# Retention, PReLU layer and mixture of experts on one core: the head's state update moved to TensorE and ScalarE, float32 products regrouped, the update cut to its diagonal blocks, and the first slot's weights given a later due time

## The chip, the core and the metric

The kernel runs on one core of a Trainium2 chip. The metric is the device time of one execution in microseconds (us); of the kernel before there are three timed runs, with a median of 981.19 us (980.25 to 981.85). One further execution was taken with the hardware profiler. TensorE is called PE here, VectorE DVE, ScalarE ACT, GpSimd POOL and SyncE SP; SP issues nearly all DMAs.

## What is computed

Three stages follow each other over 3072 tokens (4 batches of 768) with 512 features.

```
state = gamma_h * state + outer(k_t, v_t)            # per batch and head: 4 x 8 states of 64 x 64, float32
y_t   = scale * q_t @ state                          # decaying linear attention, 768 steps
h     = x @ w_in ; g = max(h,0) + alpha*min(h,0)     # 512 -> 2048
x2    = g @ w_out                                    # 2048 -> 512
e     = argmax(cosine(x2, expert_emb)/tau)           # 8 experts, top 1
out   = gate * (max(x2 @ w1[e], 0) @ w2[e])          # 512 -> 1024 -> 512, only the chosen expert
```

## The kernel before, in words

**Tiles.** The tokens are cut into 24 tiles of 128, numbered i = 4c + b: chunk c (0 to 5) of batch b (0 to 3). The recurrence is done by chunks. For each tile `att_load` fetches q, k, token-major k and v, and with each new chunk the decay factors `cqk_sb`; `att_hat` multiplies the decays in; `att_a` makes the masked scores (eight float32 products, one for each head, over 64 rows); `att_b` makes the output `y` = scores x v plus q x state (the second part only from chunk 1 on), and the update `u` = k^T v, which DVE adds to the state `st_bd`. The state lies as four 128 x 128 blocks for each batch, one for each pair of heads, of which only the two 64 x 64 blocks on the diagonal are used. `u` is computed for a pair of heads at once, four float32 products of 128 x 128, so half of each (the two blocks of one head's k with the other's v) is not read. `y` and `u` take turns in two PSUM banks (`m_ring`).

**Two kinds of tile.** Tiles 0 to 11 (`i < HALVED`) make scores x v in float32. Tiles 12 to 23 split scores and v into two float16 halves (`att_s`, three products in place of one); q x state stays float32, with the scaled state `st_y`. In `y` of these tiles the order by pair of heads is: six float16 products, one float32 product, and the next pair.

**Stages.** Called the head here: tiles 0 to 11, the conversion of the two PReLU matrices (they come in as 64-bit numbers, `convert`, `quarter`, `scale_out`, `split_out`) and the first block of h = x w_in (`mm1(0, m)`). Then the middle: blocks of 512 tokens through `mm1` and `mm2`, with tiles 12 to 23 and the splitting of the expert weights into float16 halves (written to `wsplit` in HBM) in between. In the last block the 128-token groups end one after the other; each is squared, halved (`Route.halve`), transposed by a DMA into `x2T_buf` (`Route.logits`) and multiplied with the expert embedding `emb16` on PE. After that come the expert slots: four fixed ones (t = -4 to -1, of the two most frequent experts) and then t = 0, 1, ... The weights of the slots lie in three buffers: t = -4, -3 in `stage16`, t = -2, -1 in `win16`, t = 0 in `wout16`, t = 1 in `stage16`, and so on. `load_w(t)` fetches them in four pieces of 1 MB.

**Order.** No order is written by hand. Every call is recorded (`Plan.add`; all instructions of the program are therefore issued from one line, L147) with an estimated duration (`cost`) and its dependencies. `Plan.issue` gives every node a due time `need`, counted back from the place of the PE work that depends on it, and then fills the engines' in-order queues greedily: of what can start first, the one due first. A DMA is held back until its `need` is within `AHEAD` = 60 us of the PE work just placed. `plan.bias` is added to the `need` of what is recorded under it. The added lines of the change stand in `cost`, `att_load`, `att_b`, the setup and the calls of `load_w`.

Of the kernel before, what the change touches and what calls it, by code (L numbers as in the profile page):

```python
# [14 lines left out]
AF = mybir.ActivationFunctionType  # L15
ALU = mybir.AluOpType
AX = mybir.AxisListType

B, H, S, D = 4, 8, 768, 64
NT, DM, DFF = B * S, H * D, 2048  # L20
E, F = 8, 1024
P = 128
# [5 lines left out]
KD = DM // P  # L28
# [68 lines left out]
class Plan:  # L97
# [37 lines left out]
    class Engine:  # L135
# [26 lines left out]
        def cost(self, method, kw):  # L162

            n = 1
            for d in kw["out"].shape[1:]:
                n *= d
            if "dma" in method:
                side = kw["in_"] if "indirect" not in method or kw["in_offset"] is None else kw["out"]
                n = 1
                for d in side.shape:  # L170
                    n *= d
                nb = n * mybir.dt.size(side.dtype)
                if "indirect" in method:
                    return 1040.0, 650.0, nb
                return 60.0, (1150.0 if "transpose" in method else 1000.0), nb * (1.23 if "transpose" in method else 1)
            if self.name == "PE":
                if kw["lhsT"].dtype == F32:
                    return max(214.0, 1.67 * n), 0.0, 0
                return max(27.0, 0.416 * n + 2.5), 0.0, 0
            if self.name == "ACT":  # L180
                extra = sum(93.0 for k in ("accum_out", "scale", "bias") if isinstance(kw.get(k), bass.AP))
                return (95.0 if kw["in_"].space != bass.MemoryType.PSUM else 50.0) + 0.833 * n + extra, 0.0, 0
            if self.name == "DVE":
                fast = method in ("tensor_scalar", "tensor_copy") and n > 64 and kw.get("op0") not in self.BITS
                two = method in ("scalar_tensor_tensor", "tensor_tensor") and n > 256
                return 65.0 + n * (0.52 if fast else 1.05) * (1.15 if two else 1.0), 0.0, 0
            return 140.0 + (2.13 if method == "tensor_tensor" else 1.3) * n, 0.0, 0
# [139 lines left out]
def retention_prelu_moe_kernel(ctx: ExitStack, tc, qkv, w_in, w_out, alpha, emb, tau, w1, w2,  # L327
                               c32, cqk, causal, c16, out):
    nc = tc.nc
    plan = Plan(nc)  # L330
    V, A, G, T, SP = plan.vector, plan.scalar, plan.gpsimd, plan.tensor, plan.sync
# [10 lines left out]
    def buf(name, shape, dt=F32):  # L342
        return sbuf.tile([P, *shape], dt, name=name, tag=name)
# [18 lines left out]
    cst = buf("cst", [NCOL])  # L362
    cst16 = buf("cst16", [2 * P + E], F16)
    cau = buf("cau", [P])
    alpha_sb = buf("alpha_sb", [KF])
    tau_sb = buf("tau_sb", [1])
    cqk_sb = buf("cqk_sb", [2, KD, P])

    def col(name):
        return cst[:, _COLS[name][0]:_COLS[name][1]]  # L370

    tri, ones16, base16 = cst16[:, 0:P], cst16[:, P:2 * P], cst16[:, 2 * P:]
# [14 lines left out]
    v_ring = Ring([vp_buf[:, k] for k in range(2)])  # L387
# [4 lines left out]
    first = {"qk": [room[:, 1536 * k:1536 * k + 1536].rearrange("p (a x) -> p a x", a=3) for k in range(3)] + [qk_buf, hat_buf, stage[:, 12:15]],  # L392
             "v": [room[:, 4608 + 512 * k:5120 + 512 * k] for k in range(2)] + v_ring.bufs,
             "pm": [room[:, 5632 + 512 * k:6144 + 512 * k].rearrange("p (k t) -> p k t", k=KD) for k in range(4)] + pm_ring.bufs,
             "xh": [room[:, 7680 + 512 * k:8192 + 512 * k].bitcast(F16).rearrange("p (a x) -> p a x", a=2) for k in range(3)] + xh_ring.bufs,
             }
    first = {k: Ring(v) for k, v in first.items()}
# [76 lines left out]
    qk_t, v_t, att = {}, {}, {}  # L474

    def att_load(i):
        if i % B == 0:
            SP.dma_start(out=cqk_sb, in_=cqk[i // B])
        qk_t[i] = (first["qk"] if i < B * N_ROOM else qk_ring).next() if i < HALVED else qk_buf
        SP.dma_start(out=qk_t[i], in_=qkv[i, :, 0:3])  # L480
        v_t[i] = (first["v"] if i < B * N_ROOM else v_ring).next()
        SP.dma_start(out=v_t[i], in_=qkv[i, :, 3])

    def att_hat(i):
# [77 lines left out]
    def att_b(i, early=False):  # L562

        c, b = divmod(i, B)
        j, o = divmod(i, BT)
        v = v_t.pop(i)
        hat, pr = att.pop(i)
        st = st_bd[:, b]
        y = m_ring.next()
        with plan.unit("PE"):  # L570
            for p in range(KD):
                for r in range(2):
                    h = 2 * p + r
                    if i >= HALVED:
                        for n, (a, o_) in enumerate(((0, 0), (0, 1), (1, 0))):
                            T.matmul(out=y[:, D * h:D * h + D], lhsT=p16[r][:, a, P * p:P * p + P],
                                     rhs=v16[:, o_, D * h:D * h + D], start=(r == n == 0), stop=False, skip_group_check=True)
                        continue
                    T.matmul(out=y[:, D * h:D * h + D], lhsT=pr[r][:, p, :], rhs=v[:, D * h:D * h + D],
                             start=(r == 0), stop=(r == 1 and not c), skip_group_check=True)  # L580
                if c:
                    T.matmul(out=y[:, P * p:P * p + P], lhsT=hat[:, 0, P * p:P * p + P], rhs=(st_y if i >= HALVED else st)[:, p, :],
                             start=False, stop=True, skip_group_check=True)
        if c < NCH - 1:
            u = m_ring.next().rearrange("p (k t) -> p k t", k=KD)
            with plan.unit("PE"):
                for p in range(KD):
                    T.matmul(out=u[:, p, :], lhsT=hat[:, 2, P * p:P * p + P], rhs=v[:, P * p:P * p + P],
                             start=True, stop=True)
        xh = (first["xh"] if i < B * N_ROOM else xh_ring).next()  # L590
        ss = tmp("ssx", [1])
        square_sum(y, ss, xh[:, 0, :])
        if c < NCH - 1:
            for r in (0, D):
                V.tensor_tensor(out=st[r:r + D, :, r:r + D], in0=u[r:r + D, :, r:r + D],
                                in1=st[r:r + D, :, r:r + D], op=ALU.add)
        s = tmp("sx", [1])
        pow2(ss, s, C_WIDE, hbx[:, i:i + 1])
        if o == BT - 1:
            pow2_inverse(hbx[:, i + 1 - BT:i + 1], invx[:, i + 1 - BT:i + 1], C_WIDE)  # L600
            for k in range(i + 1 - BT, i + 1):
                if k in y_inv:
                    for q in range(2):
                        V.tensor_tensor(out=invx[:, k:k + 1], in0=invx[:, k:k + 1], in1=y_inv[k][:, q:q + 1], op=ALU.mult)
        A.activation(out=xh[:, 0, :], in_=y, func=AF.Copy, scale=s)
        V.scalar_tensor_tensor(out=xh[:, 1, :], in0=y, scalar=s, in1=xh[:, 0, :], op0=ALU.mult, op1=ALU.subtract)
        if early:
            SP.dma_start(out=x_dram[i], in_=xh.rearrange("p a x -> p (a x)"))
        else:
            att_x(i, xh.rearrange("p a x -> p (a x)"))  # L610
# [376 lines left out]
    SP.dma_start(out=tau_sb, in_=tau.partition_broadcast(P))  # L987
    SP.dma_start(out=emb_sb, in_=emb)
    V.memset(st_bd, 0.0)
    V.memset(csum, 0.0)  # L990
    V.memset(ss_b, 0.0)
    V.memset(ones_b, 1.0)
# [207 lines left out]
    def load_w(t):  # L1200

        for piece in range(4):
            which, o = divmod(piece, 2)
            dst = wbuf(t)[:, 4 * piece:4 * piece + 4].rearrange("p c a x -> p (c a x)")
            cols = slice(4096 * o, 4096 * o + 4096)
            if t in (0, 1):

                SP.dma_start(out=dst, in_=wsplit[(E - 1) * t, which][:, cols])
                continue
            which_e = pre_e[t >= -NPAIR][0:1, 0:1] if t < 0 else ctl[0:1, 0, t:t + 1]  # L1210

            def load(which=which, dst=dst, which_e=which_e, cols=cols):
                ev = nc.sync.value_load(which_e, min_val=0, max_val=E - 1)
                kw = {}
                if t > 1:
                    kw = dict(cond=nc.sync.value_load(ctl[0:1, 1, t:t + 1], min_val=0, max_val=1), cond_hint=False)
                src = wsplit[bass.ds(ev, 1), which].rearrange("a p x -> p (a x)")
                nc.sync.dma_start(out=dst, in_=src[:, cols], **kw)

            plan.add("SP", load, [which_e, ctl[0:1, 1, t:t + 1], wsplit] if t > 1 else [which_e, wsplit], [dst], 250.0, 1000.0,  # L1220
                     P * 4096 * (1 if t > 1 else 2))
# [42 lines left out]
                             in_=y, in_offset=None, bounds_check=NT - 1, oob_is_err=False)  # L1264

    for t in (-NPRE, -NPAIR, 0):
        load_w(t)
    for first_t in (-NPRE, -NPAIR):
        for t in range(first_t, first_t + NPAIR):
            mm1e(t)  # L1270
        for t in range(first_t, first_t + NPAIR):
            mm2e(t)
# [84 lines left out]
```

## Time and profile before

| | before |
|---|---|
| median of the timed runs | 981.19 us (980.25 to 981.85) |
| the profiled execution | 988.65 us, span 986.9 us |
| mean granted clock of PE | 0.966 |
| busy share of the span: PE, DVE, ACT, POOL | 94 %, 58 %, 47 %, 9 % |
| HBM read, written | 200.40 MB, 51.14 MB |

The span runs from the first to the last instruction. A busy time of an engine is the time in which it carried out instructions; the PE's float32 products appear as two matmul records each, each with a load of weights of its own (PEld). A granted clock of 1.00 is 2.4 GHz and 0.50 is 1.2 GHz. "idle before ... <- X" is how long the engine stood still before an instruction and what released it.

### The profile page before, as it was taken

How to read it: one execution, taken by the hardware profiler on the slowest of the kernel's cores; microseconds unless marked ns; L12 is line 12 of the kernel's file. 1: busy time of each engine (PE TensorE's matmuls, PEld its weight loads, DVE VectorE, ACT ScalarE, POOL GpSimd, SP SyncE). 2: the span in 40 equal slices, each digit the busy share in tenths (PEclk: the TensorE clock that was granted, in tenths of full speed). 3: DMA queues.
4: the chain of work that ended last, by engine and by line, in shares of the span. 5: the costliest groups of instructions: out<-in, count | busy, mean ns of one | idle time of the engine just before them, and what ended most of it. 6: DMA issues, size and time to landing. Idle time of an engine off the chain costs nothing. (4 is left out here: it accounts for less than half of the span.)

```text
span 986.9 us, 18868 instructions
## 1 busy us (share of the span) xinstructions
PE 926.3 (94%) x7100; PEld 558.7 (57%) x7100; DVE 571.3 (58%) x1490; ACT 464.6 (47%) x825; POOL 91.4 (9%) x110
## 2 busy tenths in 40 slices
PE   6797789999999999999998999997999999989995
PEld 6775455555555555554444444446677677666663
DVE  5988989578787877796466557446422222121231
ACT  1568866577687778887576664222001101100100
POOL 0000000000200010001000100110232112132010
PEclk9797979999999999999999999998999999989998
DMA  9998723564899888888686543797687279945450
GB/s 306 305 266 254 239 102 89 161 159 119 261 277 233 221 269 269 235 229 291 197 236 229 192 156 100 298 261 153 219 195 188 72 222 341 311 114 111 63 196 25
DMA packets 129823, 201.44 MB, mean 204 GB/s; under 512 B 89726, under 2 KB 90110, under 8 KB 124608
## 3 DMA queue, kind: packets, MB, share of 16 engines
q1 hardware_dynamic: 123168, 179.42, 62.1%
q0 software_dynamic: 6560, 20.77, 6.5%
q8 instruction: 57, 0.93, 0.4%
q14 instruction: 38, 0.31, 0.1%
HBM read 200.40 MB, written 51.14 MB: 255 GB/s over the span
## 5 line engine op out<-in xcount | busy, mean ns | idle before, releaser
L147 PE MATMUL bank<-xT,win 128*128 128x512 f16 x1152 | 270.7, 386 | 7.0 <-DVE g L147 7.0
L147 PE MATMUL bank<-wout,f_buf 128*128 128x512 f16 x960 | 223.4, 381 | 0.8 <-DVE pay_buf L147 0.8
L147 PEld LDWEIGHTS <-win 128*128 128x128 f16 x1344 | 123.3, 100 | 136.9 <-issue 15.7
L147 PEld LDWEIGHTS <-f_buf 128*128 128x128 f16 x960 | 93.1, 98 | 110.9 <-issue 4.0
L147 PEld LDWEIGHTS <-stage 128*128 128x128 f16 x1440 | 89.3, 98 | 26.8 <-issue 4.2
L147 DVE SCALAR_TENSOR_TENSOR g<-g,oma,bank 128x512 f32<-128x512 f32 x96 | 71.4, 745 | 55.3 <-ACT g L147 54.6
L147 ACT ACTIVATE wout<-stage 128x1024 f16<-128x1024 f32 x64 | 67.3, 1052 | 39.2 <-DMA stage<-in_w 38.6
L147 ACT ACTIVATE st_bd<-bank 128x512 f16<-128x512 f32 x30 | 17.9, 597 | 140.5 <-PE bank L147 126.8
L147 ACT ACTIVATE g<-bank 128x512 f32<-128x512 f32 x96 | 56.4, 588 | 57.0 <-PE bank L147 56.7
L147 DVE SCALAR_TENSOR_TENSOR f_buf<-g,f_buf 128x512 f16<-128x512 f32 x80 | 55.1, 689 | 32.9 <-ACT f_buf L147 32.4
L147 POOL DMA_INDIRECT table<-pay_buf,rposi x24 | 25.6, 1066 | 473.3 <-DVE v L147 112.7
L147 PEld LDWEIGHTS <-wout 128*128 128x128 f16 x1152 | 65.9, 98 | 5.2 <-issue 2.2
L147 PEld LDWEIGHTS <-st_bd 128*128 128x128 f16 x408 | 39.8, 99 | 47.6 <-issue 2.5
L147 ACT ACTIVATE f_buf<-g 128x512 f16<-128x512 f32 x80 | 49.8, 623 | 29.0 <-DVE g L147 28.9
L147 DVE SCALAR_TENSOR_TENSOR stage<-stage,se 128x1024 f16<-128x1024 f32 x43 | 55.0, 1280 | 8.4 <-ACT stage L147 8.4
L147 PE MATMUL bank<-xT,stage 128*128 128x128 f16 x960 | 56.8, 220 | 3.2 <-issue 3.2
L147 PE MATMUL bank<-xT,wout 128*128 128x128 f16 x960 | 56.5, 220 | 1.8 <-issue 1.8
L147 DVE SCALAR_TENSOR_TENSOR st_bd<-bank,st_bd 128x512 f16<-128x512 f32 x34 | 23.3, 689 | 55.0 <-ACT st_bd L147 50.3
L147 ACT ACTIVATE stage<-stage,se 128x1024 f16<-128x1024 f32 x43 | 48.8, 1139 | 9.6 <-DMA wsplit<-stage 5.7
L147 DVE TENSOR_SCALAR xT<-bank,f_buf,cqk_sb 128x512 f32<-128x512 f32 x20 | 16.2, 810 | 62.4 <-PE bank L147 62.4
L147 PEld LDWEIGHTS <-x2T_buf 128*128 128x128 f16 x384 | 26.9, 99 | 34.1 <-DMA x2T_buf<-pay_buf 8.0
L147 PE MATMUL bank<-wout,stage 128*128 128x512 f16 (+1 forms) x200 | 44.6, 375 | 0.0
(263 smaller groups left out, 1257.8 us busy)
## 6 DMA issues: line engine op xcount, KB each, us to landing
stage<-wsplit SPq DMA_DIRECT2D x52, 1024.0 KB
wout<-wsplit SPq DMA_DIRECT2D x52, 1024.0 KB
stage<-in_w SPq DMA_DIRECT2D x64, 512.0 KB
wsplit<-stage SPq DMA_DIRECT2D x43, 512.0 KB
qk_buf<-in_qkv SPq DMA_DIRECT2D x15, 768.0 KB
wsplit<-win SPq DMA_DIRECT2D x21, 512.0 KB
f_buf<-in_w_in SPq DMA_DIRECT2D x12, 512.0 KB
vp_buf<-in_qkv SPq DMA_DIRECT2D x20, 256.0 KB
```

Of the source, the lines that this page charges most:

```text
L147: call = lambda: fn(**kw)
```

## The change

Five edits, in the order of the diff.

- The planner's estimates for float32 products on PE are set anew; they decide about order alone.
- A tile `ident` (128 x 128 identity) is made from the two triangles `cau` and `tri`, both loaded anyway.
- `att_load`: up to tile 11 only the half of the decay factors that is used there is fetched (256 KB in place of 512 KB, for chunks 0, 1 and 2); for tile 0, q and k come first, then the factors, v, and last the token-major k.
- `att_b`: for tiles 12 to 23 the four float32 products with the state stand together behind all float16 products. The update is made as eight products of 64 x 64, each head's own block. For tiles 4 to 11, a product of `ident` with the old state (128 x 512, float32) opens the update's bank, so that the sum forms in PSUM, and ACT copies the blocks to `st_bd`; for tiles 0 to 3 (state zero) ACT copies `u` alone. Tiles 12 to 19 keep DVE's addition; tiles 20 to 23 have no update.
- `load_w(0)` is recorded with a bias of 15 us.

```diff
-                    return max(214.0, 1.67 * n), 0.0, 0
+                    rows, cols = kw["lhsT"].shape[0], kw["lhsT"].shape[1]
+                    return (145.0 if rows < P else 100.0 if cols < P else 120.0 + 1.17 * n), 0.0, 0
...
     def att_load(i):
-        if i % B == 0:
-            SP.dma_start(out=cqk_sb, in_=cqk[i // B])
+        if i % B == 0 and i:
+            n = 1 if i < HALVED else 2
+            SP.dma_start(out=cqk_sb[:, 0:n], in_=cqk[i // B][:, 0:n])
...
+        if i == 0:
+            SP.dma_start(out=qk_t[i][:, 0:2], in_=qkv[i, :, 0:2])
+            SP.dma_start(out=cqk_sb[:, 0:1], in_=cqk[0][:, 0:1])
+            SP.dma_start(out=v_t[i], in_=qkv[i, :, 3])
+            SP.dma_start(out=qk_t[i][:, 2], in_=qkv[i, :, 2])
+            return
...
-                if c:
-                    T.matmul(out=y[:, P * p:P * p + P], lhsT=hat[:, 0, P * p:P * p + P], rhs=(st_y if i >= HALVED else st)[:, p, :],
+                if 0 < c and i < HALVED:
+                    T.matmul(out=y[:, P * p:P * p + P], lhsT=hat[:, 0, P * p:P * p + P], rhs=st[:, p, :],
+                             start=False, stop=True, skip_group_check=True)
+            if i >= HALVED:
+                for p in range(KD):
+                    T.matmul(out=y[:, P * p:P * p + P], lhsT=hat[:, 0, P * p:P * p + P], rhs=st_y[:, p, :],
                              start=False, stop=True, skip_group_check=True)
...
-                for p in range(KD):
-                    T.matmul(out=u[:, p, :], lhsT=hat[:, 2, P * p:P * p + P], rhs=v[:, P * p:P * p + P],
-                             start=True, stop=True)
+                add = 0 < c and i < HALVED
+                if add:
+                    T.matmul(out=u.rearrange("p k t -> p (k t)"), lhsT=ident, rhs=st.rearrange("p k t -> p (k t)"),
+                             start=True, stop=False, skip_group_check=True)
+                for h in range(H):
+                    p, r = divmod(h, 2)
+                    T.matmul(out=u[D * r:D * r + D, p, D * r:D * r + D], lhsT=hat[:, 2, D * h:D * h + D],
+                             rhs=v[:, D * h:D * h + D], start=not add, stop=True, skip_group_check=True)
...
-                V.tensor_tensor(out=st[r:r + D, :, r:r + D], in0=u[r:r + D, :, r:r + D],
-                                in1=st[r:r + D, :, r:r + D], op=ALU.add)
+                if i < HALVED:
+                    A.activation(out=st[r:r + D, :, r:r + D], in_=u[r:r + D, :, r:r + D], func=AF.Copy)
+                else:
+                    V.tensor_tensor(out=st[r:r + D, :, r:r + D], in0=u[r:r + D, :, r:r + D],
+                                    in1=st[r:r + D, :, r:r + D], op=ALU.add)
...
+    V.tensor_tensor(out=ident, in0=cau, in1=tri, op=ALU.subtract)
...
     for t in (-NPRE, -NPAIR, 0):
+        plan.bias = 15000.0 if t == 0 else 0.0
         load_w(t)
+    plan.bias = 0.0
```

## Rows read from the trace of the kernel before

**Rows 1.** Stages by windows: stretch, length, busy time of each engine (instructions), clock, DMA share, GB/s

```profile
0.00:40.00 40.00, 27.59 (x180) 25.80 (x182) 25.58 (x53) 13.11 (x21) 0.39 (x5) 0.87 0.93 299
40.00:68.00 28.00, 25.77 (x214) 20.81 (x211) 26.08 (x48) 15.43 (x24) 0.00 (x0) 1.00 1.09 332
68.00:148.00 80.00, 62.78 (x347) 39.96 (x347) 70.41 (x115) 64.13 (x94) 0.42 (x3) 0.83 0.58 189
160.00:640.00 480.00, 476.17 (x2884) 241.65 (x2883) 339.32 (x906) 324.87 (x603) 27.64 (x39) 1.00 0.71 214
```

**Rows 2.** Timeline of PE, 205 to 230 us: start, busy us, operation, count

```profile
208.03 0.34 PE L147 MATMUL bank<-v,p 128*128 128x64 f16 x6
...
208.20 0.47 PE L147 MATMUL bank<-st_y,hat_buf 128*128 128x128 f32 x2
...
209.94 1.46 PE L147 MATMUL bank<-wout,stage 128*128 128x512 f16 x6
...
214.57 1.16 PE L147 MATMUL bank<-hat_buf 64*128 64x128 f32 x16
...
215.66 1.47 PE L147 MATMUL bank<-wout,stage 128*128 128x512 f16 x6
...
220.90 1.05 PE L147 MATMUL bank<-vp_buf,hat_buf 128*128 128x128 f32 x8
...
221.79 0.81 PE L147 MATMUL bank<-wout,stage 128*128 128x512 f16 x3
```

**Rows 3.** Groups of PE by form, 160 to 640 us: busy us, mean ns, idle before

```profile
L147 PE MATMUL bank<-st_y,hat_buf 128*128 128x128 f32 x96 | 22.4, 316 | 0.0
```

**Rows 4.** The tile st_bd: its DVE additions, duration ns min/median/max, first and last

```profile
L147 DVE TENSOR_TENSOR st_bd<-bank,st_bd x40: 404/427/456, 18.8 to 335.2; 64x256 f32<-64x256 f32 x40
```

**Rows 5.** Stages by windows, instructions of the tile st_bd alone

```profile
40.00:68.00 28.00, 7.04 (x32) 4.86 (x32) 2.50 (x6) 0.00 (x0) 1.00 1.09 332
68.00:148.00 80.00, 8.85 (x32) 6.31 (x32) 4.25 (x10) 0.00 (x0) 0.83 0.58 189
```

**Rows 6.** Groups of ACT by form, 0 to 160 us

```profile
L147 ACT ACTIVATE g<-bank 128x512 f32<-128x512 f32 x17 | 10.0, 589 | 6.5 <-PE bank L147 6.4
```

**Rows 7.** DMA issues by line: form, count, KB each

```profile
cqk_sb<-in_cqk SPq DMA_DIRECT2D x6, 512.0 KB
```

**Rows 8.** Timeline of PE, 133 to 168 us: the first product with wout

```profile
154.40 2.75 PE L147 MATMUL bank<-wout,stage 128*128 128x512 f16 x12
```

**Rows 9.** Timeline of PE, 655 to 723 us

```profile
654.78 9.23 PE L147 MATMUL bank<-wout,f_buf 128*128 128x512 f16 x42
...
669.96 0.38 PE L147 MATMUL bank<-emb,x2T_buf 128*128 128x16 f16 x8 [5.95 <-DMA x2T_buf<-pay_buf]
...
670.20 5.44 PE L147 MATMUL bank<-wout,f_buf 128*128 128x512 f16 x15
...
686.05 0.35 PE L147 MATMUL bank<-emb,x2T_buf 128*128 128x16 f16 x8 [1.38 <-DMA x2T_buf<-pay_buf]
...
722.34 5.58 PE L147 MATMUL bank<-xT,wout 128*128 128x128 f16 x96
```

**Rows 10.** Timeline of SP's queue, 651 to 668 us: issue, time to issue

```profile
652.63 0.53 SPq L147 DMA_DIRECT2D wout<-wsplit  x1
...
655.93 0.39 SPq L147 DMA_DIRECT2D wout<-wsplit  x1
...
658.93 3.65 SPq L147 DMA_TRANSPOSE x2T_buf<-pay_buf  x1
...
662.68 5.15 SPq L147 DMA_TRANSPOSE x2T_buf<-pay_buf  x1
```

**Rows 11.** Stages by windows, one microsecond each

```profile
664.00:665.00 1.00, 0.01 (x1) 0.00 (x0) 0.30 (x2) 0.00 (x0) 0.00 (x0) 1.00 1.02 434
```

**Rows 12.** Timeline, 597 to 606 us: an earlier pair of transposes and its first user

```profile
599.48 5.32 SPq L147 DMA_TRANSPOSE x2T_buf<-pay_buf  x2
...
603.19 0.34 PE L147 MATMUL bank<-emb,x2T_buf 128*128 128x16 f16 x8
```

More of the change, by code (lines that the diff above doesn't have):

```diff
@@ L364, in retention_prelu_moe_kernel @@
     cau = buf("cau", [P])
+    ident = buf("ident", [P])
     alpha_sb = buf("alpha_sb", [KF])
@@ L476, in att_load @@
     def att_load(i):
-        if i % B == 0:
-            SP.dma_start(out=cqk_sb, in_=cqk[i // B])
+        if i % B == 0 and i:
+            n = 1 if i < HALVED else 2
+            SP.dma_start(out=cqk_sb[:, 0:n], in_=cqk[i // B][:, 0:n])
         qk_t[i] = (first["qk"] if i < B * N_ROOM else qk_ring).next() if i < HALVED else qk_buf
+        v_t[i] = (first["v"] if i < B * N_ROOM else v_ring).next()
+        if i == 0:
[4 more added lines that the diff above has]
+            return
         SP.dma_start(out=qk_t[i], in_=qkv[i, :, 0:3])
-        v_t[i] = (first["v"] if i < B * N_ROOM else v_ring).next()
         SP.dma_start(out=v_t[i], in_=qkv[i, :, 3])
@@ L576, in att_b @@
                             T.matmul(out=y[:, D * h:D * h + D], lhsT=p16[r][:, a, P * p:P * p + P],
-                                     rhs=v16[:, o_, D * h:D * h + D], start=(r == n == 0), stop=False, skip_group_check=True)
+                                     rhs=v16[:, o_, D * h:D * h + D], start=(h == n == 0), stop=False, skip_group_check=True)
                         continue
```

## The prediction, made before the changed kernel was built or run

> **What bounds the kernel now.** I read the stages first [rows 1]: one line for each stretch, with the busy time of every engine. From 160 to 640 us PE is busy for 476.17 of 480 us at full clock, so there any time taken off PE's instructions comes off the end. From 68 to 148 us no engine is full: DVE has 70.41 of 80 us, ACT 64.13, PE 62.78 at a mean clock of 0.83. DVE is the fullest, so its work counts first there. From 40 to 68 us DVE (26.08 of 28 us) and the DMA share (1.09) are both at their end; before 40 us it is the DMAs (0.93), with DVE at 25.58 of 40 us. The head ends where the first product with wout starts, at 154.40 us [rows 8]. The last place is the passage to the expert slots. In PE's timeline [rows 9] the reader is to see that PE runs out of work at about 664 us, stands for 5.95 us until a transposed x2T_buf arrives, and then takes 5.44 us for 15 matmuls of a form of which 42 took 9.23 us just before.
>
> **The change, part by part.**
>
> *Float32 state products side by side (tiles 12 to 23).* Today one unit of y, with four times six float16 and one float32 product, runs from 208.03 to 209.94 us: 1.91 us [rows 2]. Its first six float16 products take 208.20 - 208.03 = 0.17 us, so 0.68 us for all 24, and the four float32 ones with their changes of type have 1.23 us. The update, four float32 products of the same size side by side, takes 221.79 - 220.90 = 0.89 us [rows 2]. So each change of type costs (1.23 - 0.89)/4 = 0.085 us; of four, three go: 0.25 us for a tile. The 96 records of st_y are twelve tiles of eight [rows 3], all inside the full stretch: 12 x 0.25 = **3.0 us**. It is 0 if the extra time belongs to the operands and not to the change, and 12 x 0.34 = 4.1 us if the last change is hidden too.
>
> *Only the own blocks of the update.* No row has a product of 64 columns of weights with 64 columns moving. If the eight run one after the other, each at half of a 0.2225 us product (0.89/4), they take 0.89 us, as now; if the two halves of the array work side by side, 0.45 us. The scores use half arrays in the other direction: eight products with 128 columns moving take 215.66 - 214.57 = 1.09 us [rows 2], 1.22 times the 0.89 us of perfect pairs. So 0.45 x 1.22 = 0.55, and I add 0.2 us for going into and out of the halved array, about twice one change of type: 0.75 us, nearest to the scores' row. Gain 0.14 us for a tile, counted for the eight tiles 12 to 19 in the full stretch: **1.1 us**; bounds 8 x (0.89 - 1.09) = -1.6 and 8 x 0.44 = +3.5 us. The Trainium skill, page "TensorEngine Tiling (Array Packing)", section "Key Properties", speaks against it: a change of tiling mode, not of tile, drains TensorE. No row here shows a drain by itself; if drains ate the gain, the sum below would be 1.1 us smaller.
>
> *The state's addition moved (tiles 0 to 11).* DVE loses 24 of its 40 additions of 427 ns [rows 4]: 10.2 us in all, of which 2.50 lie in 40 to 68 us and 4.25 in 68 to 148 us [rows 5]. ACT gains 24 copies of 64 x 256 from PSUM. A copy of 512 elements takes 589 ns [rows 6]; half of it (0.29) and all of it bound the new one, I take 0.38, since part of each instruction does not depend on its length. PE gains eight products with ident, each 512 float32 columns: 4 x 0.2225 = 0.89 us at full clock, 1.78 at half; at least the 0.22 us of one float16 pass over 512 columns (9.23/42) [rows 9]. The wait that it adds, for the state as ACT left it four tiles before, q x state of the same tile has already; what is new stands behind ACT's queue and not DVE's (a rival below). For 68 to 148 us, with five tiles: DVE 70.41 - 4.25 = 66.2, ACT 64.13 + 10 x 0.38 = 67.9, PE 62.78 + 5 x (0.89 - 0.14) = 66.5 us. The fullest engine falls from 70.4 to 67.9 us, by 2.5 us; but three engines are then about equal and each waits for the others, so I take 1.5 us.
>
> *The DMAs of the first 68 us.* Three loads of decay factors shrink by half of 512 KB [rows 7]: 0.79 MB less, at 332 GB/s [rows 1] 2.4 us of the queues' time. With the 2.50 us that DVE loses in 40 to 68 us it is one gain, not two, since both are full there; I take 2.0 us. Tile 0 starts earlier, as 0.52 MB (half the factors and the token-major k) no longer stand before its first product: 1.7 us at the 299 GB/s of 0 to 40 us. SP issues one DMA more for it, 0.39 to 0.53 us of its queue by the plain loads of [rows 10]. The stream behind it is bound by bytes, so 0.5 us is left. The making of ident is one more DVE instruction, smaller than an addition of the state, in a stretch where DVE has 14 us idle.
>
> The head together: 1.5 + 2.0 + 0.5 = **4.0 us**. Bounds: 8 x 0.75 = 6.0 us of loss, if PE's added work all stands in the way and nothing else helps, and 10.2 us of gain, if all that DVE loses counts. The new estimates reorder the head's queues; I have no row for that, and leave it inside these bounds.
>
> *The first slot's weights later.* SP issues two of the four pieces, 1 MB each, at 652.63 and 655.93 us; two transposes follow at 658.93 and 662.68 and take 3.65 and 5.15 us to issue [rows 10]. The DMAs still move 434 GB/s from 664 to 665 us [rows 11], loads and not transposes. The earlier pair, with no loads ahead, had its first user 603.19 - 599.48 = 3.7 us after the first issue [rows 12]; the later one 669.96 - 658.93 = 11.0 us. Due 15 us later, the two pieces come behind this pair: 2.1 MB at 434 GB/s are 4.9 us less. A stall of about 1 us is left, between none (658.93 + 3.7 lies before 664) and 2.1 us (if the second transpose, whose data are ready 3.5 us after the first's, counts). With so short a stall the clock stays up: 5.44 - 15 x 0.22 = 2.1 us come back. **7.0 us**. The four are plain DMAs with nothing else on SP. They are needed from 722.34 us on [rows 9]; 15 us later than 655.93 leaves 50 us, so that end is covered. What they can hit is the next pair of transposes, where PE waits 1.38 us today [rows 9]: if all four pieces now stood ahead of it, 4.9 us would be lost again. Bounds 2.1 and 5.95 + 2.1 = 8.1 us. The Trainium skill, page "DMA: Bandwidth & Descriptors", section "Where 436 GB/s comes from", puts loads from HBM at about 358 GB/s for a core. The trace differs with its 434 GB/s, and the measurement decides; by the page's figure the pieces would be worth 5.9 us and the sum would be 1 us larger.
>
> **Sum.** 3.0 + 1.1 + 4.0 + 7.0 = 15.1 us. The profiled execution took 988.65 us and would take 973.5; it is 7.5 us above the median of 981.19 us, and I take the same gain off that: **966 us**.
>
> **Rivals.**
> - *The loads hit the transposes all the same* (that edit doesn't do what it says). For it: the planner fills SP's queue whenever a load may go, and the second pair of transposes follows closely. Against: 15 us is longer than the 11.0 us from the first issue to its user. The gain of 7.0 us goes: 973 us.
> - *The head gives nothing.* ACT and PE get what DVE loses, and three engines at 66 to 68 of 80 us wait for one another. 970 us. Both together: 977 us.
> - *The head gives all of DVE's time*, 10.2 us in place of 4.0: 960 us. Against it stands the DMA share of 1.09 in 40 to 68 us.
> - *Slower.* The update's bank is one of two that all tiles share, and it now comes free when ACT has copied it. PE's queue is in order, so a product for that bank holds everything behind it. Price for each of the tiles 4 to 11: 0.89 for ident, 0.76 for two copies, 0.59 for one ACT instruction ahead of them, 2.24 us, 17.9 us in all, against 11.1 us from the other parts: 988 us. It decides from (11.1 + 2)/8 = 1.6 us a tile. Against it: PE has 17 us idle in 68 to 148 us, and DVE, which frees the bank today, is the fuller engine.
>
> **How the numbers follow.** Forecast 0.48, loads hit the transposes 0.15, head gives nothing 0.17, both 0.05, head gives all 0.07, slower 0.08. The range 957 to 977 us takes in every case but the slower one and the outer halves of its neighbours. 0.2 % is 2 us, about what a measurement of this kernel can tell from no change: faster 0.88, same 0.04 (the upper part of "both"), slower 0.08.
>
> **What would show it.** In y of tiles 12 to 23: 24 float16 products and then eight float32 records, 1.65 us in place of 1.91. An update of about 0.75 us, and in tiles 4 to 11 before it a 128 x 512 float32 product of 0.9 us. The first product with wout near 150 us. Loads of wout from wsplit behind the first two transposes of x2T_buf, a stall below 2 us there, and no stretch at half clock after it. I am wrong if the first product with wout is not earlier, or if the stall only moves to the second pair.

## The result, and the profile after

The changed kernel takes **972.93 us** (median of four runs, 970.79 to 975.04); the kernel before, run beside it, 981.52 us (980.25 to 985.52). The ratio is **0.9888** with a 95 % interval of [0.9855, 0.9922]: faster by 1.1 %, inside the forecast's range, but by 8.6 us where 15.1 were forecast. Two more groups of runs on other chips gave 0.9863 [0.9834, 0.9892] and 0.9889 [0.9854, 0.9924], which is 13.2 and 11.8 us. Executions more than 1.5 % above the fastest of their kernel are left out of medians and ratios.

The profiled execution took 975.04 us, its span is 973.3 us. First its stages, in the columns and stretches of [rows 1] (length, busy time of PE, PEld, DVE, ACT, POOL with their counts, clock, DMA share, GB/s):

```profile
40.00:68.00 28.00, 25.62 (x206) 18.03 (x205) 20.99 (x38) 18.10 (x30) 0.00 (x0) 0.94 0.97 292
68.00:148.00 80.00, 67.95 (x438) 40.77 (x437) 70.81 (x119) 68.67 (x109) 2.71 (x3) 0.91 0.59 198
160.00:640.00 480.00, 475.79 (x2972) 237.50 (x2971) 337.45 (x901) 323.85 (x602) 35.79 (x44) 1.00 0.71 217
```

From 160 to 640 us PE is as full as before: what it saves there shows as later work coming earlier, not as idle time. From 40 to 68 us DVE fell from 26.08 to 20.99 us and the DMA share from 1.09 to 0.97. From 68 to 148 us DVE did not fall: though ten additions of the state are gone from it [rows 5], it has 119 instructions in place of 115, so work that used to come later has moved up, and PE rose from 62.78 to 67.95 us.

PE's timeline of the same kernel (start, busy us, operation, count), in order the product with ident, the first product with wout, an update, and a unit of y; they answer to [rows 2, 8]:

```profile
122.85 1.02 PE L147 MATMUL bank<-st_bd,ident 128*128 128x512 f32 x2
123.81 0.69 PE L147 MATMUL bank<-vp_buf,qk_buf 128*64 128x64 f32 x16
...
147.37 5.34 PE L147 MATMUL bank<-wout,stage 128*128 128x512 f16 x24
...
198.73 0.69 PE L147 MATMUL bank<-vp_buf,hat_buf 128*64 128x64 f32 x16
199.35 2.76 PE L147 MATMUL bank<-xT,win 128*128 128x512 f16 x12
201.95 0.86 PE L147 MATMUL bank<-v,p 128*128 128x64 f16 x24
202.65 1.14 PE L147 MATMUL bank<-st_y,hat_buf 128*128 128x128 f32 x8
203.62 2.10 PE L147 MATMUL bank<-wout,stage 128*128 128x512 f16 x9
```

A unit of y now takes 203.62 - 201.95 = 1.67 us, the update 199.35 - 198.73 = 0.62, the ident product 123.81 - 122.85 = 0.96. ScalarE's copies of the state, as a group (busy us, mean ns, idle before):

```profile
L147 ACT ACTIVATE st_bd<-bank 64x256 f32<-64x256 f32 x24 | 9.0, 376 | 2.6 <-PE bank L147 2.4
```

Now the passage to the expert slots. PE's timeline after, to be held against [rows 9] (in brackets the idle time before, and what ended it):

```profile
658.66 0.37 PE L147 MATMUL bank<-emb,x2T_buf 128*128 128x16 f16 x8 [4.45 <-DMA x2T_buf<-pay_buf]
658.89 5.75 PE L147 MATMUL bank<-wout,f_buf 128*128 128x512 f16 x15
...
675.38 0.35 PE L147 MATMUL bank<-emb,x2T_buf 128*128 128x16 f16 x8 [1.70 <-DMA x2T_buf<-pay_buf]
...
710.09 2.12 PE L147 MATMUL bank<-xT,wout 128*128 128x128 f16 x35
```

and SP's queue after, against [rows 10] (issue, time to issue):

```profile
644.46 0.36 SPq L1245 DMA_DIRECT2D win<-wsplit  x1
644.86 0.43 SPq L147 DMA_DIRECT2D wout<-wsplit  x1
646.13 0.34 SPq L1245 DMA_DIRECT2D win<-wsplit  x1
646.57 0.45 SPq L147 DMA_DIRECT2D wout<-wsplit  x1
649.14 8.40 SPq L147 DMA_TRANSPOSE x2T_buf<-pay_buf  x2
```

The stall is still there, and so are the 15 slow matmuls: 5.75 us, with a granted clock of 0.57 over them, mostly the lower of the two levels. By windows (columns as in the stages above):

```profile
658.90:664.50 5.60, 5.60 (x22) 2.07 (x19) 3.82 (x29) 1.77 (x5) 0.00 (x0) 0.57 0.54 187
```

The reason stands in SP's queue: two pieces of the first slot's weights (the rows named wout; those named win are weights of the slots before) still go out ahead of the transposes, at 644.86 and 646.57.

To see where the time went I cut each trace at three marks: the first product with wout, the moment at which PE runs out of work before the first emb product (its start less its idle time), and the first product of slot 0 (bank<-xT,wout). I use two profiled executions of the kernel before (span 986.9 us, and a second one, 980.3) and three of the changed one (973.3, 968.4, 973.1), since single executions differ by some microseconds:

| stretch, us | before | mean | after | mean | gain | forecast |
|---|---|---|---|---|---|---|
| head, to the first wout product | 154.4, 152.9 | 153.7 | 147.4, 145.9, 146.9 | 146.7 | 7.0 | 4.0 |
| middle, to PE out of work | 509.6, 509.4 | 509.5 | 506.8, 504.0, 504.6 | 505.2 | 4.3 | 4.1 |
| passage, to slot 0 | 58.3, 55.5 | 56.9 | 55.9, 54.8, 58.5 | 56.4 | 0.5 | 7.0 |
| slots, to the end of the span | 264.6, 262.5 | 263.5 | 263.2, 263.7, 263.1 | 263.4 | 0.1 | 0 |

The middle is as forecast, the head gave more, the passage next to nothing. The gains add up to 11.9 us and not to 8.6, because these are five single executions; the three groups of timed runs gave 8.6, 13.2 and 11.8 us.

### The profile page after: what moved, and what is told of

It is laid out like the page before. It is cut to its first block, busy times and chain, and to the rows that moved or that the text cites. A ratio compares the mean times of both kernels' runs of the same rounds, so it can differ in the third digit from the quotient of the medians.

```text
span 973.3 us, 19219 instructions
## 1 busy us (share of the span) xinstructions
PE 922.6 (95%) x7276; PEld 548.5 (56%) x7276; DVE 561.1 (58%) x1467; ACT 471.9 (48%) x849; POOL 97.6 (10%) x110
## 5 line engine op out<-in xcount | busy, mean ns | idle before, releaser
L147 PE MATMUL bank<-xT,win 128*128 128x512 f16 x1152 | 266.9, 382 | 6.9 <-DVE g L147 6.9
L147 ACT ACTIVATE st_bd<-bank 128x512 f16<-128x512 f32 (+1 forms) x54 | 26.9, 499 | 141.6 <-PE bank L147 127.1
L147 POOL DMA_INDIRECT table<-pay_buf,rposi x24 | 28.6, 1194 | 443.3 <-DVE f_buf L147 122.8
L147 PE MATMUL bank<-xT,stage 128*128 128x128 f16 x960 | 56.4, 219 | 2.2 <-issue 2.2
L147 PE MATMUL bank<-wout,st_bd 128*128 128x512 f16 x192 | 45.8, 397 | 0.8 <-issue 0.8
L147 ACT ACTIVATE x2T_buf<-bank 128x512 f16<-128x512 f32 x14 | 8.4, 597 | 75.2 <-PE bank L147 52.7
```

Source lines behind the costliest of these rows:

```text
L147: call = lambda: fn(**kw)
```

## The experiments

They ran in three groups; each time stands beside the kernel before on the same chip, and ratios are to that.

**The kernel before again, one profile.**

> The kernel before, profiled once more. Its first profile was of an execution of 988.65 us, 7 us above its median. Theory A (an execution that was slow somewhere by chance, at PE's half clock or by DMAs): 980 to 985 us, the first product with wout still at 154 us within 1.5, the stall before the first product with emb at the passage again 5 to 6 us. Rival B (the profile itself costs 7 us): 987 to 990 us.

It took 982.1 us, span 980.3: theory A. The first product with wout came at 152.94 us; the stall was 4.57 us, a little below the 5 to 6 that were expected. So the profiled execution on which the forecast rests was a long one, and I had been right to take the gain off the median.

**First slot's weights without a bias.**

```
-        plan.bias = 15000.0 if t == 0 else 0.0
+        plan.bias = 0.0
```

> The changed kernel with the first slot's weights due as before (no bias); all else as changed, and every engine's order the same but for SP, where one load of wout goes back in front of one load of win. Theory A (the bias only exchanged these two loads, both still stand ahead of the first pair of transposes of x2T_buf): the same time as the changed kernel within 1.5 us, 972 to 974 us, and a stall of 4 to 6 us before the first product with emb at the passage. Rival B (the bias did bring its forecast share of up to 7 us): 977 to 980 us.

975.36 us (972.0 to 978.7), ratio 0.9903 [0.9865, 0.9941]. PE waits 5.51 us, then 15 matmuls take 5.80. SP's queue of this kernel:

```profile
642.72 0.53 SPq L147 DMA_DIRECT2D wout<-wsplit  x1
644.40 1.52 SPq L1245 DMA_DIRECT2D win<-wsplit  x2
646.01 0.68 SPq L147 DMA_DIRECT2D wout<-wsplit  x1
647.07 9.45 SPq L147 DMA_TRANSPOSE x2T_buf<-pay_buf  x2
```

The same two pieces stand ahead of the same two transposes as in the changed kernel; only the first of them has changed places with a load of win. The order of PE is the same in both. So the 15 us moved one load by one place. The stall is as in theory A, and the time agrees with it as far as it can be told: 975.36 us lies 1.4 us above theory A's 974 and below rival B's 977, and the interval of the ratio overlaps that of the changed kernel.

**The weights 55 us later.**

```
-        plan.bias = 15000.0 if t == 0 else 0.0
+        plan.bias = 55000.0 if t == 0 else 0.0
```

> The changed kernel with a bias of 55 us in place of 15 on the first slot's weights, so that by the planner's order all four loads of wout come behind both pairs of transposes of x2T_buf. Theory A (the 1 MB loads ahead of the transposes make the stall): the stall before the first product with emb falls from 4.45 us to below 1.5, the second one (1.70 us) to below 1, the 15 matmuls after it take 3.3 us and not 5.75, together 5 to 6.5 us less: 966 to 968 us. Rival B (the two loads of win, which stay ahead, or the transposes' own time make the stall): 971 to 974 us, stall still above 3 us. Rival C (the weights now come too late for slot 0): a new wait of PE before the first product of x2T with wout, 973 us or more.

970.24 us (962.5 to 971.44), ratio 0.9832 [0.9793, 0.9872], where bias 0 in the same group had 975.36. SP's queue and PE's timeline of this kernel:

```profile
644.34 1.54 SPq L1245 DMA_DIRECT2D win<-wsplit  x2
649.05 13.35 SPq L147 DMA_TRANSPOSE x2T_buf<-pay_buf  x4
662.45 1.54 SPq L147 DMA_DIRECT2D wout<-wsplit  x3
```

```profile
653.96 0.34 PE L147 MATMUL bank<-emb,x2T_buf 128*128 128x16 f16 x8
654.17 3.40 PE L147 MATMUL bank<-wout,f_buf 128*128 128x512 f16 x15
...
700.23 4.92 PE L147 MATMUL bank<-win,st_bd 128*128 128x512 f16 x22 [3.47 <-DVE st_bd L147]
704.99 1.22 PE L147 MATMUL bank<-xT,wout 128*128 128x128 f16 x19
```

Now all four transposes go ahead of the pieces of wout. The stall is gone, the 15 matmuls take 3.40 us at a clock of 1.00, and the second stall is gone too. That is theory A's passage: the two loads of win still go ahead of the transposes, so rival B is out. But the time lies between the two theories, and 3.47 us come back at 700 us, as a wait for DVE's st_bd (the tile is used again in the slots, for their hidden activations). DVE's timeline says what it was doing:

```profile
693.12 0.22 DVE L147 SCALAR_TENSOR_TENSOR ids<-f_buf,cqk_sb 128x1 int32<-128x1 int32 x1 [8.86 <-DMA f_buf<-table,cqk_sb]
...
699.36 0.22 DVE L147 SCALAR_TENSOR_TENSOR ids<-f_buf,cqk_sb 128x1 int32<-128x1 int32 x1 [5.42 <-DMA f_buf<-table,cqk_sb]
699.49 1.28 DVE L147 SCALAR_TENSOR_TENSOR st_bd<-bank,st_bd 128x512 f16<-128x512 f32 x2
```

It stands for 8.86 and 5.42 us at a tiny operation on a slot's row numbers, which waits for gathered rows, with the st_bd operations that PE needs queued behind it. In the same execution the first product with wout came only at 150.31 us, though this edit touches only loads issued after 640 us: single executions of one head can differ by 4 us.

**The same, with the row numbers out of the way.** Their operation is recorded behind the slot's output y and writes over the weight that y reads, so it has to follow y.

```
-            ids = tmp("ids", [1], I32)
-            V.scalar_tensor_tensor(out=ids, ...)
         y = y_ring.next()
         V.tensor_scalar(out=y, in0=ps, ...)
+            ids = g[:, DM:DM + 1]
+            V.scalar_tensor_tensor(out=ids, ...)
-        plan.bias = 15000.0 if t == 0 else 0.0
+        plan.bias = 55000.0 if t == 0 else 0.0
```

> First slot's weights due 55 us later instead of 15, and the row numbers of a slot (ids) computed behind that slot's scaled output y, so that in VectorE's queue they no longer stand ahead of the st_bd operations. Theory A (in the 55 us run the wait of 3.47 us at 700 us is VectorE standing at ids for the gathered rows, with st_bd queued behind): the wait goes, the 15 products on emb still start without a stall, and the time is 3 to 3.5 us under the 55 us run's distance from the changed kernel, 966 to 969 us. Rival B (the wait was for something that comes late anyhow, the gathered rows or the pieces of wout): a wait of 3 us or more stays at 697 to 705 us, and the time is that of the 55 us run, 970 to 972.

**966.19 us** (962.25 to 968.66), ratio 0.9830 [0.9801, 0.9858]; the changed kernel in the same group (its expectation below) 969.96. PE's timeline of this kernel:

```profile
653.03 0.36 PE L147 MATMUL bank<-emb,x2T_buf 128*128 128x16 f16 x8 [0.99 <-DMA x2T_buf<-pay_buf]
...
689.86 10.52 PE L147 MATMUL bank<-win,st_bd 128*128 128x512 f16 x48
700.22 2.23 PE L147 MATMUL bank<-xT,wout 128*128 128x128 f16 x37
```

The 48 products on st_bd run through, and the passage takes 700.2 - 652.0 = 48.2 us, against 51.0 with 55 us alone and 54.8 for the changed kernel in the same group (54.8 to 58.5 in its three executions). Theory A for the wait: it was DVE's queue, and it is gone. As times, 966.19 lies 3.8 us under the changed kernel beside it; against the 55 us run, on another chip, the ratios (0.9830 and 0.9832) tell no difference, so the 2.8 us between those two are shown by the traces alone.

> The changed kernel unedited, as the control of this group. It should lie at 972 to 976 us; what the others are worth is read against it and not against the kernel before alone.

969.96 us (965.86 to 972.49): a little better than expected.

**Float32 products put back between the float16 ones.**

```
-                if 0 < c and i < HALVED:
+                if c:
                     T.matmul(out=y[:, P * p:P * p + P], lhsT=hat[:, 0, P * p:P * p + P],
-                             rhs=st[:, p, :], ...)
+                             rhs=(st_y if i >= HALVED else st)[:, p, :], ...)
```

> The changed kernel with the four float32 products with st_y of tiles 12 to 23 put back between the float16 ones; no engine's order but PE's differs, and PE's only inside these units. Theory A (each change between float16 and float32 costs 0.085 us of PE, and PE is full there): a unit takes 1.91 us in place of 1.67, twelve tiles, 2.9 us slower than the changed kernel: 975 to 977 us. Rival B (other waits take the time up): within 1 us of the changed kernel.

976.01 us (969.92 to 979.6), ratio 0.9905 [0.9872, 0.9938]. The time lies where theory A had it, but it tells nothing: bias 0, on the same chip and with the same order of PE but for these units, has 975.36. The traces tell it. The middle, cut as in the table, takes 507.9 us, against 505.7 with bias 0 and 504.0 to 506.8 in the changed kernel, and the unit of y in PE's timeline shows why:

```profile
201.91 0.34 PE L147 MATMUL bank<-v,p 128*128 128x64 f16 x6
202.09 0.47 PE L147 MATMUL bank<-st_y,hat_buf 128*128 128x128 f32 x2
...
203.82 2.11 PE L147 MATMUL bank<-wout,stage 128*128 128x512 f16 x9
```

203.82 - 201.91 = 1.91 us again, as in [rows 2], so theory A. With the same operands in both orders, the 0.24 us belong to the changes of type.

**The update in full blocks.**

```
-                for h in range(H):
-                    p, r = divmod(h, 2)
-                    T.matmul(out=u[D * r:D * r + D, p, D * r:D * r + D], ...)
+                for p in range(KD):
+                    T.matmul(out=u[:, p, :], lhsT=hat[:, 2, P * p:P * p + P], rhs=v[:, P * p:P * p + P], ...)
```

> The update of the state as four products of 128x128 blocks again, with both heads' cross blocks, instead of eight of 64x64, in a plan charged the same; all else as changed. Theory A (0.27 us a tile on TensorE, as the profile of after shows against before): tiles 12 to 23 add 2.2 us over the 8 with an update behind the middle's start, and the head, where TensorE waits for VectorE, adds 0 to 1: 975 to 976 against 973. Rival B (the small products' saving is hidden by waits for VectorE and ScalarE): no difference that can be measured, 972 to 974.

974.29 us (970.33 to 977.4), ratio 0.9917 [0.9891, 0.9944], 4.3 us over its control. In the timeline its update starts at 199.35 and the next product at 200.24:

```profile
199.35 1.05 PE L147 MATMUL bank<-vp_buf,hat_buf 128*128 128x128 f32 x8
200.24 2.11 PE L147 MATMUL bank<-xT,win 128*128 128x512 f16 x9
```

0.89 us again. The times are theory A's in direction; eight tiles explain 8 x 0.27 = 2.2 of the 4.3 us. The profiled execution was the shortest of the six and shows neither part: its middle takes 504.9 us, as in the changed kernel, and PE waits 1.0 us from 160 to 640 us in place of 1.8 to 4.0. So what the smaller update takes off PE is shown, and what of it reaches the end is not; rival B is not excluded.

**The state added by VectorE again.**

```
-                add = 0 < c and i < HALVED
+                add = False
...
-                if i < HALVED:
-                    A.activation(out=st[...], in_=u[...], func=AF.Copy)
-                else:
-                    V.tensor_tensor(...)
+                V.tensor_tensor(...)
```

> In tiles 0 to 11 the state is added by VectorE again (40 additions of about 427 ns) and the product with the identity and ScalarE's copies are left out; all else as changed. Theory A (the head's gain comes mostly from VectorE's freed time): the first product with wout comes at 150 to 152 us instead of 147, time 976 to 979. Rival B (the gain comes from the loads placed earlier and behind less): 147 to 148 us, time as the changed kernel's. Rival C (the identity products on TensorE and the copies on ScalarE hold the head back): 143 to 146 us, about 969.

973.04 us (970.31 to 976.19), ratio 0.9904 [0.9875, 0.9933], 3.1 us over its control; the first product with wout at 150.33 us, where the control has 145.87. The mark is 4.5 us later, as in theory A, the price in time smaller than its 976 to 979. One mark of one execution does not decide it: in the 55 us run it came at 150.31 with the changed kernel's head, where all other runs with that head have 145.87 to 147.37. Rival C, which wanted an earlier mark and 969 us, is out. (Of the 40 additions of the expectation 24 belong to tiles 0 to 11.)

**The loads in their old places; then both undone; then the old prices.** In the first, cqk is loaded whole and ahead of the tiles, and tile 0's own order of loads is undone as well (not printed); the second also has VectorE's additions as above; the third only gives the planner its old estimates.

```
-        if i % B == 0 and i:
-            n = 1 if i < HALVED else 2
-            SP.dma_start(out=cqk_sb[:, 0:n], in_=cqk[i // B][:, 0:n])
+        if i % B == 0:
+            SP.dma_start(out=cqk_sb, in_=cqk[i // B])
```

```
-                    return (145.0 if rows < P else 100.0 if cols < P else 120.0 + 1.17 * n), 0.0, 0
+                    return max(214.0, 1.67 * n), 0.0, 0
```

> The changed kernel unedited once more, as the control of this group: 970 to 973 us, first product with wout at 146 to 148 us.

> The loads of q, k, v and of the masks cqk in their old places, one batch of tiles ahead of use in the record, with cqk ahead of the tiles and v not held back; the state is still added by TensorE. Theory A (the loads give the part of the head's gain that the additions do not: before's first product with wout at 153 to 154 us, without the additions on TensorE 150, changed 146 to 147): first product with wout at 149 to 150 us, 3 us more than the control, 973 to 976. Rival B (the loads are worth nothing once VectorE is free, what is left over comes from the planner's new prices): as the control, within 1 us.

> The state added by VectorE in tiles 0 to 11 and the loads in their old places, both at once; the heads' own blocks, the products side by side and the first slot's weights as changed. Theory A (additions and loads together are the whole of the head's gain): first product with wout at 152 to 155 us as in the kernel before, and the time 976 to 980. Rival B (they overlap, either one alone brings it): 149 to 151 us, 973 to 975, the time of the additions alone.

> The planner's old prices for the small products of TensorE, and so another order of the work; no operation changes. Theory A (the prices alone move little): first product with wout within 1.5 us of the control, time within 3 us of it. Rival B (the new prices carry the rest of the head's gain): first product with wout at 149 to 151 us, 973 to 976.

| kernel | median us | ratio to before | first wout product |
|---|---|---|---|
| changed, control | 973.72 | 0.9889 [0.9854, 0.9924] | 146.88 |
| old loads | 981.5 | 0.9959 [0.9929, 0.9988] | 153.03 |
| old loads and VectorE's additions | 977.21 | 0.9929 [0.9909, 0.9949] | 151.39 |
| old prices | 981.1 | 0.9953 [0.9919, 0.9987] | no like mark |

The parts of the head don't add up. With the state on TensorE the old loads cost 7.8 us, two to three times what theory A gave them; with VectorE's additions as well the loss is only 3.5 us, about that of the additions alone (3.1). For the pair, the time lies where theory A had it, but the mark, 151.39, lies between the two theories and short of the 153 to 154 of the kernel before. So neither theory is shown. Each edit lets the planner write another order for the whole head; that this is why the parts do not add up is likely, and not shown.

The old prices cost 7.4 us where I expected under 3 (in its profiled order a lone product with wout comes early, so the mark can't be used). PE runs out of work at the transposes at 657.7 us, where the control does at 651.5. PE's waits name part of it. From 160 to 640 us PE waits 6.6 us (for DVE's roh 2.8, ss_b 1.8, pay_buf 1.3, v 0.7). The control waits 2.3 us, and 0.9 of it for roh; the two executions of before wait 2.8 and 2.4 us for roh, as with the old prices. In the first 160 us PE waits 25.2 us, within the 22.7 to 25.7 of the three executions of the changed kernel. So 4.3 of the 6.2 us that are lost before the transposes are waits of the middle, and none is shown in the head.

## Why the prediction was right, and where it was wrong

**Right in sign and range, 7 us off in size.** The forecast was 966 us; the kernel takes 972.93. The step that failed is the last term: "Due 15 us later, the two pieces come behind this pair". They did not. That the time lies inside the range all the same is partly luck: the head gave 3 us more than forecast, in a way that I had not foreseen.

- *First slot's weights, 7.0 us: failed.* I read a due time as a place in the queue. The planner lets a DMA go once its due time is within 60 us of the work just placed; that number stands in the description of the kernel, and I did not set the 15 us against it. In the planner's own arithmetic (it follows from the code of `Plan.issue`, no run measures it) the two pieces are due 32 and 27 us after the work just placed when they go without a bias, and 47 and 42 with 15 us: still inside the 60. The run without a bias shows that the edit only changed two neighbours on SP. This is the rival "the loads hit the transposes all the same" (973 us, chance 0.15). What I held against it, that 15 us is longer than 11.0, compared the wrong two things. The price of the stall was right: with the pieces behind the transposes the passage takes 48.2 us in place of 54.8 on the same chip, 6.6 us against 7.0 (that kernel has the row numbers moved too; by the medians of the times the two differ by 3.8 us). Set against the trace of the changed kernel above, the stall gives 4.45 - 0.99 = 3.5, the 15 matmuls at full clock (3.40 us, as with 55 us alone) 5.75 - 3.40 = 2.35 (forecast 2.1) and the second stall 1.7 us. What I had not seen is the next wait: "50 us, so that end is covered" looked at the weights alone, while with the transposes early the gathered rows became late, in front of st_bd on DVE. One reading under the stall's lower bound was wrong too: the user at 603.19 us is not that of the pair of transposes issued from 599.48 us on [rows 12]. Each group of eight emb products uses one transpose, in order; SP's queue and PE's timeline of the kernel before:

```profile
588.22 1.24 SPq L147 DMA_TRANSPOSE x2T_buf<-pay_buf  x1
593.02 1.24 SPq L147 DMA_TRANSPOSE x2T_buf<-pay_buf  x1
...
599.11 0.34 PE L147 MATMUL bank<-emb,x2T_buf 128*128 128x16 f16 x8
...
607.28 0.35 PE L147 MATMUL bank<-emb,x2T_buf 128*128 128x16 f16 x8
```

 So 603.19 belongs to the transpose of 593.02, and the pair's first user came at 607.28, 7.8 us after its issue, behind other work of PE. The 3.7 us, and with it the bound of no stall at all, had no row behind it. With 55 us the first user came 653.96 - 649.05 = 4.9 us after the issue, with no wait of PE before it.
- *Float32 products side by side, 3.0 us: right.* 12 x (1.91 - 1.67) = 2.9 us, and the operands' share is ruled out.
- *Own blocks of the update, 1.1 us: right in kind, half the size.* 0.62 us in place of the 0.75 that I took: 8 x 0.27 = 2.2 us of PE's time (what of it reaches the end the run with full blocks leaves open). The 0.2 us that I added for going into and out of the halved array were too much: by the scores' factor alone the sum was 0.55. The Trainium skill, page "TensorEngine Tiling (Array Packing)", section "Key Properties", has TensorE drain at a change of tiling mode. By the trace at most 0.62 - 0.45 = 0.17 us over my estimate of perfect pairs is left for that and for all else; the scores' factor, from which the 0.55 comes, may hold such a cost already.
- *Head, 4.0 us: right in sign, too small.* The mark moved by 7.0 us in the mean of the table; the one execution at 150.31 shows how far a single one can stray. The pieces were priced well (ScalarE's copy 376 ns against 0.38 us, the ident product 0.96 against 0.89 us), but the sum by the fullest engine was not the way in which the gain came. DVE stayed as full as it was from 68 to 148 us; what fell is what PE waited for. Waits of PE in the first 160 us, after (total, times, longest):

```profile
PE bank L147 <- DVE wout L147: 11.1, 4, 7.0
PE bank L147 <- DVE g L147: 6.9, 5, 3.5
PE bank L147 <- DVE xh L147: 4.0, 1, 4.0
PE bank L147 <- ACT st_bd L147: 2.5, 2, 1.3
```

 and of the kernel before:

```profile
PE bank L147 <- DVE wout L147: 14.5, 6, 7.7
PE bank L147 <- DVE xh L147: 8.3, 3, 5.1
PE bank L147 <- DVE g L147: 7.0, 3, 4.4
PE bank L147 <- DVE tot L147: 1.8, 1, 1.8
```

 Together they fell from 31.6 to 24.5 us, by 7.1, which is the gain at the mark. I had left the new estimates "inside these bounds" without a price; undone by themselves they cost 7.4 us, as much as any edit of the head, though what the trace shows of it lies in the middle. How the 7.0 us split between additions, loads, blocks and prices stays open, because undoing them one at a time and in pairs gives sums that disagree.
- *The slower rival: out.* It wanted 1.6 us a tile of PE waiting for ScalarE's copies. PE waits 2.5 us for them in the whole head, and 5.8 us, 0.7 a tile, in the 55 us run, the one with the late mark.

That 966.19 us, the time of the version with 55 us and the row numbers moved, is the forecast's number is partly luck: there the passage gave what was forecast, but the head more, and the kernel before took 983.18 us on that chip, not the 981.19 from which I had counted.

## What to carry to other kernels

Where a planner with a window decides when a load goes, a later due time does nothing until it leaves the window: read the queue that comes out, before pricing the move. When a stall is removed, follow the in-order queue of each engine that feeds the next stretch for an operation that waits for something late with needed work behind it; moving one tiny operation gave back a wait of 3.5 us. And in a head where three engines are about equally full and a planner orders the work anew after each edit, measured prices need not add up: old loads cost 7.8 us and VectorE's additions 3.1, both together 3.5. Such edits are to be measured together, not summed.

## What the runs showed of the hardware that I had not expected

- Eight float32 products of 64 columns of weights with 64 columns moving, in the two halves of the array by turns, take 0.62 us. By the estimate from the full blocks they would take 0.89 one after the other and 0.45 in perfect pairs: 1.38 times perfect pairs, where the scores' half products in the other direction take 1.22 times [rows 2].
- The same transpose holds SP's queue for 1.2 us or for five. The tile x2T_buf from 560 to 720 us (duration ns min/median/max, first and last start), before and with 55 us:

```profile
L147 SPq DMA_TRANSPOSE x2T_buf<-pay_buf x8: 1232/1298/5146, 588.2 to 679.2; - x8
L147 SPq DMA_TRANSPOSE x2T_buf<-pay_buf x8: 1232/1232/1290, 579.7 to 661.1; - x8
```

 With 55 us, where two loads of win stand ahead of them, none takes more than 1.29 us. Behind two pieces of wout and two loads of win the two transposes took 3.65 and 5.15 us before [rows 10], and 2.53 (at 649.14) and 5.17 us (at 652.38) after. The merged rows of 13.35 us for four (with 55 us) and 5.32 us for two [rows 12] are mostly time in which SP stood between them: with 55 us it waited for DVE (longest 4.8 us, for pay_buf), in the earlier pair for PE (longest 2.7 us).
- After a stall the clock can fall, but not by the stall's length alone. After 4.45 us without work the clock granted over the next 5.6 us was 0.57; after 0.99 us it stayed at 1.00 (653.2 to 656.5 us with the row numbers moved). After 3.23 us in the second execution of the changed kernel it fell, after 3.24 us with VectorE's additions it did not (stretches behind the stall, columns as in the stages above):

```profile
653.30:659.40 6.10, 6.10 (x25) 2.28 (x23) 3.82 (x29) 1.77 (x5) 0.00 (x0) 0.54 0.52 177
...
660.50:663.80 3.30, 3.30 (x24) 1.52 (x21) 2.92 (x27) 1.53 (x5) 0.00 (x0) 1.00 0.85 113
```

 So how much of the 15 matmuls' slow time comes back with a shorter stall is not settled by the stall's length; what sets it stays open.
